# Emitting the engine programs into the main body instead of a Block, in a one-core transformer-block kernel

## The chip, the cores and the metric

One Trainium2 chip, one of its cores. The metric is the device time of one execution in microseconds (us). The "span" of a trace is shorter: from the first to the last instruction of the kernel that the profiler recorded. Both numbers exist for every timed run.

## The reference, cut to what matters

A block with adaptive layer norm: linear attention, then a SwiGLU feed-forward, on 2048 rows of 1024 features in bfloat16.

```python
mod = (silu(c) @ w_mod)                # six rows: sa, ca, ga, sb, cb, gb
h = layernorm(x) * (1 + ca) + sa
x = x + ga * linear_attention(h, A_wqkv, A_wo)
h = layernorm(x) * (1 + cb) + sb
x = x + gb * ((silu(h @ w_gate) * (h @ w_up)) @ w_down)   # 1024 -> 3584 -> 1024
```

The arithmetic is not touched by the change. The last result is stored to memory in small pieces, and the kernel must not be over before the last piece has landed.

## The kernel before

The kernel first records all operations in a list and works out the semaphore waits between them. It then emits one program per engine:

```python
    def emit(self, sems, engines):
        for eng, ops in self.by_eng.items():
            deco = engines[eng]

            def body(e, ops=ops, eng=eng):
                for op in ops:
                    for k, v in op.waits:
                        e.wait_ge(sems[k], v)
                    if op.fn is None:
                        continue
                    r = op.fn(e)
                    ...            # cut: semaphore increments
            deco(body)
```

The `deco` of each engine comes from a Block. A Block gives every engine a body of its own, to which it branches, and joins all five engines behind an all-engine barrier at its end:

```python
    with ExitStack() as es:
        block = es.enter_context(nc.Block())
        ...                        # cut: tiles and the whole list of operations
        P.wait_for("sp", out_ops)  # SyncE waits for all 33 stores

        counters = P.resolve()
        sems = {}
        for key in counters:
            sems[key] = es.enter_context(nc.semaphore(key.replace(":", "_")))
        engines = {"pe": block.tensor, "act": block.scalar, "dve": block.vector, "pool": block.gpsimd,
                   "sp": block.sync}
        P.emit(sems, engines)
```

The last row tile is finished in three pieces so that little is left after the last matmul. The last piece is 128 columns wide: one addition on VectorE, then a store of 128 x 256 bytes.

```python
                        if c0 > 0:
                            P.dve("tensor_tensor", out=xs, in0=PS[:, pb, c0:c1], in1=xs, op=ALU.add)
                        ...        # cut: the wider pieces
                        out_ops.append(P.dma("out", ov[:, st, nh * 512 + c0:nh * 512 + c1], xs))
```

## Time and profile before

| | before |
|---|---|
| time, median of the first three runs | 831.32 us |
| span of the traced run | 829.4 us |
| TensorE busy | 824.0 us, 99% |
| start of the last matmul | 826.60 us |
| issue of the last store | 827.17 us |
| last landing of that store | 828.67 us |
| end of the span | 829.44 us |

The head of the profile page of the kernel before gives the span, the number of instructions and each engine's busy time with its share of the span and its number of instructions:

```profile
span 829.4 us, 10017 instructions
## 1 busy us (share of the span) xinstructions
PE 824.0 (99%) x4083; PEld 378.4 (46%) x4083; DVE 312.0 (38%) x665; ACT 197.6 (24%) x336; POOL 39.8 (5%) x57
...
```

TensorE is the limit and it hardly ever pauses. The chain of waits that ended last (start, duration, what) shows what stands before and after its work:

```profile
...
1.71 4.21 DMA xres<-in_A_x_dram
...
8.76 818.08 PE ps L176 x4069
826.83 0.02 issue
826.86 0.29 DVE xres L176
```

There are 8.76 us of lead-in, one unbroken block of matmuls, and a tail. The waits of SyncE in the last microseconds of the kernel before (who waited for whom: us in total, times, longest) say what the tail is:

```profile
...
engine line waited for: us in total, times, longest us
...
SPq L286 <- DMA out_dram<-xres: 1.2, 1, 1.2
SPq L286 <- PEq L286: 0.5, 1, 0.5
```

SyncE waits 1.2 us for the last store, and then 0.5 us more in the Block's closing barrier. (The releaser's name is a guess of the profile: the barrier is released by GpSimd, as the records below show.) The view of the DMA traffic from 827.1 us to the end of the span (packets, MB and share of the 16 engines per queue; then KB and us from issue to landing of the stores issued in it) has a store that lands in 1.5 us:

```profile
...
## 3 DMA queue, kind: packets, MB, share of 16 engines
q1 hardware_dynamic: 288, 0.13, 19.3%
issues: line engine op xcount, KB each, median us to landing
out_dram<-xres SPq DMA_DIRECT2D x1, 32.0 KB, 1.5
```

The single instruction records at the end of the trace, shortened (start us, duration us, engine, record):

```
827.174  0.333  SyncE    issue of the last store
828.684  0.041  SyncE    branch, after the wait for all stores
828.865  0.013  SyncE    drain, counts up the gather semaphore
828.903  0.017  GpSimd   gather complete
829.334  0.017  GpSimd   release
829.376  0.017  SyncE    released; the others up to 829.439
```

### The profile page before, as it was taken

How to read it: one execution, taken by the hardware profiler on the slowest of the kernel's cores; microseconds unless marked ns; L12 is line 12 of the kernel's file. 1: busy time of each engine (PE TensorE's matmuls, PEld its weight loads, DVE VectorE, ACT ScalarE, POOL GpSimd, SP SyncE). 2: the span in 40 equal slices, each digit the busy share in tenths (PEclk: the TensorE clock that was granted, in tenths of full speed). 3: DMA queues.
4: the chain of work that ended last, by engine and by line, in shares of the span. 5: the costliest groups of instructions: out<-in, count | busy, mean ns of one | idle time of the engine just before them, and what ended most of it. 6: DMA issues, size and time to landing. Idle time of an engine off the chain costs nothing.

```text
span 829.4 us, 10017 instructions
## 1 busy us (share of the span) xinstructions
PE 824.0 (99%) x4083; PEld 378.4 (46%) x4083; DVE 312.0 (38%) x665; ACT 197.6 (24%) x336; POOL 39.8 (5%) x57
## 2 busy tenths in 40 slices
PE   8999999999999999999999999999999999999998
PEld 4544444454444444444444444444444444444444
DVE  5797986756955521121221111122111111221111
ACT  4757641323242111011111101111110111111011
POOL 1010000000130000030000003000000300000000
PEclk9999999999999999999999999999999999999999
DMA  9969655928397996700455570045557004553000
GB/s 320 288 151 229 149 159 172 202 102 304 60 258 225 259 267 174 192 25 14 128 150 155 150 188 28 15 126 153 153 153 187 26 18 125 154 151 86 0 26 26
DMA packets 199245, 119.28 MB, mean 144 GB/s; under 512 B 57880, under 2 KB 182944, under 8 KB 199200
## 3 DMA queue, kind: packets, MB, share of 16 engines
q1 hardware_dynamic: 199184, 118.65, 52.7%
q8 instruction: 32, 0.52, 0.3%
q14 instruction: 13, 0.11, 0.0%
q10 hardware_dynamic: 16, 0.00, 0.0%
HBM read 100.67 MB, written 4.33 MB: 127 GB/s over the span
## 4 chain that ended last, share of the span: by engine, by line
PE 99%; DMA 1%; DVE 0%; ACT 0%; SPq 0%; issue 0%
PE ps L176 99%; DMA xres<-in_A_x_dram 1%; DVE stats L176 0%; ACT xres L176 0%; SPq L176 0%; DVE xres L176 0%; DVE mv L176 0%; DVE nmr L176 0%
## 5 line engine op out<-in xcount | busy, mean ns | idle before, releaser
L176 PE MATMUL ps<-h2t,gug 128*128 128x512 bf16 x896 | 211.7, 379 | 0.0
L176 PE MATMUL ps<-h2t,guu 128*128 128x512 bf16 x896 | 211.7, 379 | 0.0
L176 DVE TENSOR_TENSOR at<-sg,ps 128x512 bf16<-128x512 bf16 x112 | 77.1, 688 | 282.7 <-PE ps L176 281.1
L176 ACT ACTIVATE sg<-ps 128x512 bf16<-128x512 f32 x112 | 66.9, 597 | 309.7 <-PE ps L176 309.7
L176 PEld LDWEIGHTS ps<-h2t,guu 128*128 128x128 bf16 x896 | 87.5, 98 | 105.8
L176 PEld LDWEIGHTS ps<-h2t,gug 128*128 128x128 bf16 x896 | 87.4, 98 | 105.7
L176 PE MATMUL ps<-wd_a,at 128*128 128x512 bf16 (+1 forms) x512 | 112.4, 378 | 0.0
L176 PE MATMUL ps<-ht,wqk 128*128 128x512 bf16 x512 | 111.7, 379 | 0.0
L176 PE MATMUL ps<-wd_b,at 128*128 128x512 bf16 (+1 forms) x384 | 85.0, 378 | 0.0
L176 PEld LDWEIGHTS ps<-wd_a,at 128*128 128x128 bf16 x512 | 50.0, 98 | 59.8
L176 DVE TENSOR_TENSOR ut<-att,gb_b 128x512 bf16<-128x512 bf16 (+1 forms) x32 | 13.8, 430 | 167.5 <-ACT att L176 167.5
L176 PEld LDWEIGHTS ps<-ht,wqk 128*128 128x128 bf16 x512 | 49.4, 98 | 58.8
L176 ACT ACTIVATE att<-ps 128x512 bf16<-128x512 f32 (+1 forms) x32 | 17.4, 591 | 182.1 <-PE ps L176 182.1
L176 PEld LDWEIGHTS ps<-wd_b,at 128*128 128x128 bf16 x384 | 37.5, 98 | 44.7
L176 PE MATMUL ps<-pk,xres 128*128 128x512 bf16 x256 | 56.5, 379 | 0.0
L176 PE MATMUL ps<-mw,pqt 128*128 128x512 bf16 x256 | 56.3, 379 | 0.0
L176 POOL TENSOR_SCALAR h2t<-h2t,modcol 128x512 bf16<-128x512 bf16 x32 | 26.4, 841 | 383.0 <-DMA h2t<-xn 383.0
L176 ACT ACTIVATE e<-ps 128x512 bf16<-128x512 f32 x56 | 33.1, 603 | 31.7 <-PE ps L176 20.5
L176 PEld LDWEIGHTS ps<-mw,pqt 128*128 128x128 bf16 x256 | 24.8, 98 | 30.3 <-DVE xres L176 0.4
L176 PEld LDWEIGHTS ps<-pk,xres 128*128 128x128 bf16 x256 | 24.8, 98 | 30.0 <-issue 0.4
L176 ACT ACTIVATE junk<-xres 128x1024 bf16<-128x1024 bf16 x24 | 25.4, 1058 | 35.1 <-DVE xres L176 34.9
L176 DVE SCALAR_TENSOR_TENSOR xres<-ps,xres 128x512 bf16<-128x512 f32 x32 | 21.4, 689 | 12.3 <-PE ps L176 11.7
(107 smaller groups left out, 346.0 us busy)
## 6 DMA issues: line engine op xcount, KB each, us to landing
gug<-in_B_w_gate_dram SPq DMA_DIRECT2D x56, 512.0 KB, 3.9
guu<-in_B_w_up_dram SPq DMA_DIRECT2D x56, 512.0 KB, 5.2
xres<-in_A_x_dram SPq DMA_DIRECT2D x20, 256.0 KB, 7.8
rb<-recip_den SPq DMA_DIRECT2D x8, 512.0 KB, 11.5
stgx<-in_w_mod_dram SPq DMA_DIRECT2D x2, 2048.0 KB, 7.8
wd_a<-in_B_w_down_dram SPq DMA_DIRECT2D x4, 1024.0 KB, 7.8
out_dram<-xres SPq DMA_DIRECT2D x31, 128.0 KB, 1.7
xres<-in_A_x_dram SPq DMA_DIRECT2D x3, 1024.0 KB, 14.0
```

The source lines that it names most:

```text
L176: return getattr(e, method)(**kw)
```

## The change

The intent: drop the Block, so that there is no branch into a body, no branch out of it, and above all no all-engine barrier at the end. SyncE's wait for all stores, which was already there, becomes the end of the kernel.

```diff
@@ emit
-            deco(body)
+            body(deco)
@@ kernel
-        block = es.enter_context(nc.Block())
@@ end
-        engines = {"pe": block.tensor, "act": block.scalar, "dve": block.vector, "pool": block.gpsimd,
-                   "sp": block.sync}
+        engines = {"pe": nc.tensor, "act": nc.scalar, "dve": nc.vector, "pool": nc.gpsimd, "sp": nc.sync}
```

Compared engine by engine, the programs are the same except for the branches and the barrier.

## The prediction

> **What bounds the kernel now.** TensorE. The profile page gives PE 824.0 us busy of a span of 829.4 us (99%) at a granted clock of 1.0, and the chain that ended last is 818.08 us of matmuls without a break (8.76 to 826.83 us), with 8.76 us of lead-in (a load of x, its statistics and normalisation) and 2.61 us of tail. The time of a run (831.32 us) is 1.9 us more than the span. The change can touch only lead-in, tail and those 1.9 us.
>
> **What the change does.** The order of instructions, compared engine by engine, is the same apart from names: no load, matmul, wait or store moves. What goes is (a) one branch per engine on entry, (b) one on exit, (c) one all-engine barrier at the end: a drain and a semaphore wait on four engines, a drain, a gather and a release on POOL. Next to nothing is added: SyncE already waits for all stores before; that wait is carried by its exit branch, and becomes a plain semaphore wait.
>
> **Cost of each, from the instruction records of the trace.**
> - Entry: no branch is recorded. SyncE's start-up semaphore wait is at 0.703 us and its first DMA issue at 0.785 us, so at most some 0.05 us can hide there; the start-up barrier stays. [...] This trace shows no such stall at entry, so I count 0.
> - Exit: the last store is issued at 827.174 us and SyncE's branch runs at 828.684 us, when the store has landed. Then come the branch (0.041 us), SyncE's drain at 828.865, POOL's gather at 828.903, POOL's release at 829.334, and the other engines' waits, the last ending at 829.439. After landing that is 0.755 us, all on the critical path. A plain wait takes 0.02 to 0.04 us (such records take 0.017 to 0.041). Saved: about 0.72 us.
> - The other engines' drains end by 827.20 us: off the path.
> - [...] SyncE still comes last to it, so I expect it unchanged, a few tenths either way. No view of this trace shows it.
>
> **Prediction.** 831.32 - 0.72 = 830.6 us, 0.09% faster; range 830.1 to 831.1 us. Faster by over 2%: 0.002; within 2%: 0.995; slower by over 2%: 0.003. The three runs before differ by 0.23 us, so the gain is only just visible.
>
> **What the profile would show.** Instruction count 10017 falls by 11 to 10006. The barrier's records at the end are gone; the last record is SyncE's semaphore wait right after the last store lands, so the tail shrinks from 2.6 to about 1.9 us. Span about 828.7 us. The block of matmuls stays 818.1 us within 0.3 us, the lead-in 8.8 us within 0.3 us. Time minus span stays about 1.9 us.
>
> **What would make it wrong.** The runtime's end takes back what the barrier gave (time minus span grows by 0.7 us: no gain), or starts its work early on the idle engines (gain over 0.72 us). The start-up loads land differently by some tenths, which moves the whole block. Instruction fetches shift by a few instructions on every engine; TensorE could gain or lose a fraction of a us.

The 1.9 us between the span and the time (831.32 - 829.4) are the "it" to which SyncE "still comes last". That they follow SyncE was the assumption; the trace shows only that SyncE is the last engine to end its work (its branch at 828.684 us, the other engines' drains over by 827.20 us). "The runtime's end", and "the runtime's end code" in the expectations, are names for whatever comes behind the kernel.

## The result, and the profile after

The changed kernel is correct. Its median is 831.59 us (830.65 to 831.82, 6 runs), against 831.22 us (830.89 to 831.43, 6 runs) for the kernel before. A ratio in this document is the one recorded with each result, made from the fast runs; it is not quite the ratio of the medians. Here it is 1.0002, with a 95% interval from 0.9989 to 1.0015: the same. The predicted 0.7 us are not there.

The head of the page, and the chain, of the changed kernel:

```profile
span 830.2 us, 10006 instructions
## 1 busy us (share of the span) xinstructions
PE 824.5 (99%) x4083; PEld 378.9 (46%) x4083; DVE 312.5 (38%) x665; ACT 197.5 (24%) x336; POOL 40.1 (5%) x57
...
```

```profile
...
8.79 12.47 DMA wsa<-in_w_mod_dram
21.26 0.04 issue
21.31 806.13 PE ps L176 x3932
827.44 0.02 issue
827.46 0.29 DVE xres L176
```

The 11 instructions are gone, as predicted (ten of the barrier and SyncE's exit branch; no other branch is recorded). The span, however, grew from 829.4 to 830.2 us. The block of matmuls ends 0.61 us later (827.44 instead of 826.83 us). Matched one by one, its matmuls are 0.64 us ahead of the kernel before at 8 us and 0.61 us behind from 46 us on: 0.44 us of this is lost at 21 us, where they wait for a load (`wsa`), and the rest in several smaller steps. The tail should have shrunk from 2.61 us to about 1.9 us; it grew to 2.79 us (830.23 - 827.44). SyncE's waits at the end show where:

```profile
...
engine line waited for: us in total, times, longest us
...
SPq L247 <- DMA out_dram<-xres: 2.1, 1, 2.1
```

The barrier's wait is gone, but the wait for the last store went from 1.2 to 2.1 us. The DMA traffic from 827.7 us to the end of the span:

```profile
...
q1 hardware_dynamic: 288, 0.13, 17.8%
q14 instruction: 1, 0.01, 0.9%
issues: line engine op xcount, KB each, median us to landing
out_dram<-xres SPq DMA_DIRECT2D x1, 32.0 KB, 2.4
```

There is a guest: one packet on q14, an instruction fetch, and the same 32 KB store now takes 2.4 us to land. A close-up of the changed kernel from 828.95 to 829.55 us, in 40 slices of 15 ns (bytes are counted where a packet starts):

```profile
...
GB/s 0 0 0 546 0 0 0 0 0 0 0 0 0 0 0 0 0 0 0 0 0 0 0 0 0 0 0 17 17 17 17 17 17 17 17 0 0 0 0 0
DMA packets 10, 0.01 MB, mean 17 GB/s; under 512 B 9, under 2 KB 9, under 8 KB 9
...
```

The fetch starts in the fourth slice. Nothing starts in the next 23. Then come exactly eight packets of the store, one per slice. The ninth packet under 512 B is one of 4 bytes; a store has 16 of these, as it has 16 landings. The packet records give the numbers:

```
                                       before           changed
first packet of the last store         828.001          828.609
instruction fetch, 8192 bytes, q14     830.057-830.550  829.003-829.364
last packets of the last store         no gap           8 of 128 from 829.361
15th and 16th of its 4-byte packets    828.241, .262    828.868, 829.474
15th of the store's 16 landings        828.654          829.254
16th landing                           828.668          830.199
```

Eight of 128 packets are one sixteenth of the store. Fifteen of the sixteen landings are on time, and the last comes 0.95 us after the fifteenth. In the kernel before, a fetch of the same size came too, but at 830.06 us, after the barrier and outside the span. The times fit a fetch that stands in the way of these packets: eight packets wait until 3 ns before the fetch ends (829.361 and 829.364 us), one of the 16 landings is late, and SyncE's wait ends only after it (the wait's record is at 830.215 us, the 16th landing at 830.199 us). The trace does not name the DMA engine of a packet, so that fetch and packets shared one is inferred from these times, and one time does not quite fit (see "What stays open").

A third thing changed: time minus span fell from 1.78 us (831.22 - 829.44) to 1.25 us (831.48 - 830.23), and it is low in every run of the changed kernel (1.22 to 1.32 us in six runs).

So the difference of the two traced runs, +0.26 us (831.48 - 831.22), is the sum of four terms:

| term | before | changed | difference |
|---|---|---|---|
| start to the issue of the last store | 827.17 | 827.78 | +0.61 |
| issue to last landing | 1.49 | 2.42 | +0.92 |
| last landing to end of span | 0.77 | 0.03 | -0.74 |
| end of span to end of time | 1.78 | 1.25 | -0.53 |

### The profile page after: what moved, and what is told of

Same layout as the page of the kernel before. It is cut to its first block, busy times and chain, and to the rows that moved or that the text cites. A ratio compares the mean times of both kernels' runs of the same rounds, so it can differ in the third digit from the quotient of the medians.

```text
span 830.2 us, 10006 instructions
## 1 busy us (share of the span) xinstructions
PE 824.5 (99%) x4083; PEld 378.9 (46%) x4083; DVE 312.5 (38%) x665; ACT 197.5 (24%) x336; POOL 40.1 (5%) x57
## 4 chain that ended last, share of the span: by engine, by line
PE 97%; DMA 2%; SPq 1%; issue 0%; DVE 0%
PE ps L176 97%; DMA wsa<-in_w_mod_dram 2%; SPq L176 1%; DVE xres L176 0%
```

## The experiments

All kernels gave correct results. Each was timed in five rounds beside the kernel before on the same chip, and one run of each was traced. The time from the start to the last store's issue scatters by about 1 us from trace to trace, whatever the end of the kernel looks like. So the most telling number is what follows that issue.

Main theory, "collision": with no barrier to hold the idle engines, one of them runs on into the code behind the kernel, and its instruction fetch takes a DMA engine that still has its share of the last store to move. Rival, "chance": landings of a store scatter, and the fetch is a bystander. A second question is which engine fetches. I first thought ScalarE, because its program seemed to end close before a fetch boundary: in the trace of the changed kernel fetches of 8192 bytes start after the 65th, 193rd, 320th and 448th of ScalarE's 560 records (at 47.90, 121.84, 307.37 and 583.40 us), about 128 apart, so the next would be due some 16 records past its end. (That these four are ScalarE's is inferred from the spacing; the trace does not name a fetch's engine.)

The table collects all traces: us from the issue of the last store to its last landing; from there to the end of the span; from there to the end of the time; and the sum. The last column is where the last small instruction fetch (q14) came, relative to the issue of the last store.

| kernel | landing | span end | time end | sum | fetch |
|---|---|---|---|---|---|
| before | 1.49 | 0.77 | 1.78 | 4.05 | +2.88 |
| changed | 2.42 | 0.03 | 1.25 | 3.70 | +1.22 |
| rep_after | 2.46 | 0.03 | 1.25 | 3.75 | +1.30 |
| end_barrier | 1.50 | 0.62 | 1.80 | 3.93 | +2.71 |
| hold_all | 1.49 | 0.08 | 2.11 | 3.68 | +3.03 |
| hold_act | 1.50 | 0.04 | 1.62 | 3.16 | +2.77 |
| hold_dve | 2.38 | 0.05 | 1.38 | 3.81 | +1.15 |
| hold_pool | 1.48 | 0.04 | 2.14 | 3.66 | +3.04 |
| hold_pe | 1.49 | 0.08 | 1.74 | 3.31 | +2.94 |
| pad_act | 2.41 | 0.03 | 1.25 | 3.69 | +1.08 |
| pad_pool | 1.48 | 0.03 | 1.25 | 2.76 | none near |
| rep_pad_pool | 1.48 | 0.03 | 1.25 | 2.76 | none near |
| pad_pool128 | 2.43 | 0.03 | 1.26 | 3.72 | +1.27 |
| before_pad_pool | 1.48 | 0.42 | 1.72 | 3.62 | none near |

### rep_after: the changed kernel again

No edit.

> The changed kernel again, for a second trace. Collision theory (with nothing to hold the idle engines, one runs on into the code behind the kernel, and its 8192-byte instruction fetch occupies one DMA engine while that engine still has its sixteenth of the last store to move): a fetch on q14 again starts some 1.0 to 1.5 us after the last store's issue, one of the 16 landings of that store comes about 0.9 us after the other 15, and the last wait ends about 2.4 us after the issue of the last store. Chance theory (landings of a store just scatter): the wait ends about 1.5 us after the issue, as in the kernel before. Time minus span 1.25 us in both.

Measured: median 830.89 us against 831.27 us of before, ratio 0.9994 (0.9980 to 1.0007). The fetch came again, 1.30 us after the issue; 15 landings by 829.144 us and the 16th at 830.131 us. So the collision repeats. Only the start differed enough to give another median.

### end_barrier: the barrier back, still no Block

```diff
         P.emit(sems, engines)
+        nc.all_engine_barrier()
```

> The changed kernel with an all-engine barrier added at the end, still without a Block. If entry is free and only the end matters: like the kernel before, that is the last store lands 1.5 us after its issue, about 0.75 us of barrier after it, time minus span about 1.8 us, the q14 fetch after the end of the span, and the time within 0.3 us of the kernel before. If the removed entry branches matter: TensorE's block of matmuls keeps the changed kernel's later start (last matmul at 827.4 us) and the time stays some 0.4 us over that of before.

Measured: median 831.72 us against 831.27 us, ratio 1.0002 (0.9989 to 1.0014). SyncE's waits at the end of this kernel:

```profile
...
SPq L247 <- DMA out_dram<-xres: 1.2, 1, 1.2
SPq L1173 <- PEq L1173: 0.5, 1, 0.5
```

These are the two lines of the kernel before. The landing takes 1.50 us, and time minus span is 1.80 us. SyncE's first DMA issue is at 0.785 us, as in the kernel before, and at 0.786 us in the changed kernel. (That the last matmul starts at 826.59 us, before at 826.60 us, is luck: this time scatters by about 1 us.) So what the change does lies in the closing barrier, but for the exit branch; the entry branches are worth nothing that can be seen. The exit branch is worth about 0.12 us: SyncE's drain comes 0.06 us after its wait here (828.682 to 828.741), and 0.18 us after its branch began in the kernel before (828.684 to 828.865).

### hold_all: no barrier, but nobody may run on

```diff
         P.wait_for("sp", out_ops)
+        for e in ("pe", "act", "dve", "pool"):
+            P.wait_for(e, out_ops)
```

(In the kernel these are four lines.)

> The changed kernel with TensorE, ScalarE, VectorE and GpSimd each also waiting for all stores as their last instruction: no gather and release, but nobody can run ahead. Collision theory: the fetch comes after the landing, the store lands 1.5 us after its issue, the span ends within 0.1 us of the landing (about 0.72 us shorter than with the barrier), time minus span goes back to about 1.8 us, and the time is about 0.7 us under that of before. Chance theory: the landing scatters as in the changed kernel. If idle engines' running ahead saved nothing outside the span: time minus span stays at 1.25 us.

Measured: median 830.84 us against 831.27 us, ratio 0.9994 (0.9981 to 1.0007). The landing is back at 1.49 us, and the fetch comes after it (3.03 us after the issue). The span ends 0.08 us after the landing, as the collision theory wanted. But time minus span rose to 2.1 us (2.04 to 2.16 in five runs), more than the 1.8 us expected. Of the 0.72 us expected, the end gives 0.37 us (4.05 - 3.68). So the time outside the span depends on when the engines end their programs: 1.25 us with SyncE alone held until the landing (the changed kernel's trace), 2.11 us with all five held.

### hold_act, hold_dve, hold_pool, hold_pe: one engine held

```diff
         P.wait_for("sp", out_ops)
+        P.wait_for("act", out_ops)     # or "dve", "pool", "pe"
```

> The changed kernel with ScalarE alone also waiting for all stores. If ScalarE makes the colliding fetch (its fetches are 128 instructions apart, and the next one falls some 15 instructions past its end), or stands before the fetching engine in the runtime's end code: the fetch moves behind the landing, the store lands 1.5 us after its issue, and the time is about 0.9 us under the changed kernel's colliding runs. If another engine makes it and does not depend on ScalarE: the fetch stays about 1.2 us after the issue of the last store and the wait still ends 2.4 us after it.

> The changed kernel with VectorE alone also waiting for all stores. Holding ScalarE alone moved the fetch behind the landing. If ScalarE fetches and stands first in the runtime's end code, holding VectorE changes nothing there: fetch at about 1.2 us after the issue of the last store, 16th landing 0.9 us late, wait ends 2.4 us after the issue. If the fetch (which came 1.2 to 1.3 us after VectorE's last instruction in both traces of the changed kernel) comes only once VectorE too has reached the end code, it moves behind the landing here as well: wait ends 1.5 us after the issue, span ends with it, time minus span about 1.6 us.

> The changed kernel with GpSimd alone also waiting for all stores; GpSimd has been idle since 650 us and is the other engine that may be near a fetch boundary. If GpSimd makes the fetch, it moves behind the landing (wait ends 1.5 us after the issue of the last store). If ScalarE makes it and does not need GpSimd: still 2.4 us and the late 16th landing.

> The changed kernel with TensorE alone also waiting for all stores. Holding ScalarE or GpSimd moved the fetch behind the landing, holding VectorE did not; in the colliding traces the fetch came 1.4 to 1.65 us after TensorE's last matmul. If GpSimd reaches its fetch only after TensorE has reached the end code: the fetch moves behind the landing, wait ends 1.5 us after the issue of the last store. If TensorE does not matter: fetch about 1.2 us after the issue, wait ends 2.4 us after it.

Measured: medians 830.71 (hold_act, before 831.27), 830.95 (hold_dve, before 831.52), 830.63 (hold_pool, before 831.52) and 830.43 us (hold_pe, before 831.35). The ratios are 0.9990, 0.9996, 0.9990 and 0.9991, with intervals that all contain 1. The traces are clearer. The DMA traffic from just before the last store to the end of the span, for hold_act and then for hold_dve:

```profile
...
q1 hardware_dynamic: 288, 0.13, 28.7%
issues: line engine op xcount, KB each, median us to landing
out_dram<-xres SPq DMA_DIRECT2D x1, 32.0 KB, 1.5
```

```profile
...
q1 hardware_dynamic: 288, 0.13, 18.0%
q14 instruction: 1, 0.01, 1.0%
issues: line engine op xcount, KB each, median us to landing
out_dram<-xres SPq DMA_DIRECT2D x1, 32.0 KB, 2.4
```

Holding ScalarE, GpSimd or TensorE moves the fetch behind the landing (2.77, 3.04 and 2.94 us after the issue), and the store lands in 1.5 us. Holding VectorE does not (1.15 us), and eight packets wait again (a gap from 828.093 to 828.556 us, the fetch ending at 828.560 us). So in these runs the fetching engine gets to its fetch only when TensorE, ScalarE and GpSimd have all arrived in the code behind the kernel. It is one of the three, but the holds alone cannot say which. The holds also price being late: time minus span is 1.27 us when only SyncE is late (the changed kernel), and 1.35 with VectorE, 1.63 with ScalarE, 1.76 with TensorE and 2.12 us with GpSimd held as well (means of five runs). In the last three the fetch, too, comes after the landing, and what part of the price is the fetch's was not separated.

### pad_act and pad_pool: move the fetch instead

Nothing is held at the end. The code of one engine is made 24 instructions longer, at a place where that engine is idle, so that the boundary at which it fetches falls elsewhere.

```diff
                 if ch == 0 and ft < 8:
                     macc(STGX[1], ft)
+                if ch == 3 and ft == 0:
+                    for _ in range(24):
+                        P.add("act", lambda e: e.drain(), tag="pad")    # or "pool"
```

> The changed kernel with 24 drains added to ScalarE's program at the start of the last chunk's FFN, where ScalarE is idle four fifths of the time; they shift its code by 24 instructions and nothing is held at the end. Collision theory with ScalarE fetching at every 128th instruction: the fetch falls inside the kernel, before its last activations, none near the last store; the store lands 1.5 us after its issue, the span ends within 0.04 us of it, time minus span is 1.25 us or less, and from the issue of the last store to the end of the time it takes about 2.8 us instead of 4.05 (before) and 3.7 (changed): about 1.2 us under before. If another engine fetches: nothing moves, 3.7 us.

> The same 24 drains in GpSimd's program instead: the placebo if ScalarE makes the fetch (wait ends 2.4 us after the issue of the last store, one landing 0.9 us late, 3.7 us to the end of the time), and the cure if GpSimd makes it (1.5 us and 2.8 us).

Measured: here my belief in ScalarE fell. pad_act did move a fetch of ScalarE into the kernel (to 803.65 us), but the colliding one stayed, at 828.265 us. Its landing took 2.41 us; median 830.87 us against 831.52 us, ratio 0.9993 (0.9980 to 1.0005). The placebo was the cure. pad_pool: median 829.83 us against 831.52 us, ratio 0.9979 (0.9966 to 0.9991). This is the first kernel whose interval excludes 1. The DMA traffic of pad_pool at its end, and then from 649.7 to 652 us, where the drains run:

```profile
...
q1 hardware_dynamic: 288, 0.13, 28.2%
issues: line engine op xcount, KB each, median us to landing
out_dram<-xres SPq DMA_DIRECT2D x1, 32.0 KB, 1.5
```

```profile
...
## 3 DMA queue, kind: packets, MB, share of 16 engines
q14 instruction: 1, 0.01, 1.0%
```

The fetch left the end of the kernel and turned up beside GpSimd's drains, at 650.83 us. At that time GpSimd has nothing more to do, and no store is waited for. It is GpSimd that fetches. From the issue of the last store to the end of the time it now takes 2.76 us, instead of 4.05 us (before) and 3.70 us (changed).

### pad_pool128: as many drains as lie between two fetches

The same edit with `range(128)`.

> The changed kernel with 128 drains in GpSimd's program instead of 24. With 24 the fetch on q14 came at 650.8 us, beside the 13th drain. Collision theory, fetches at every 128th instruction: one fetch again beside the 13th drain at about 650.8 us, the next 128 instructions later, which is again in the runtime's end code: the collision returns, wait ends 2.4 us after the issue of the last store, 3.7 us from that issue to the end of the time. If the drains themselves and not the place of the boundary made the gain: 1.5 us and 2.7 us as with 24.

Measured: one fetch at 651.36 us beside the drains, and another at 828.52 us, again in the store's way. Eight packets wait until 828.824 us, the fetch ending at 828.827 us:

```profile
...
q14 instruction: 1, 0.01, 0.8%
issues: line engine op xcount, KB each, median us to landing
out_dram<-xres SPq DMA_DIRECT2D x1, 32.0 KB, 2.4
```

The median is 830.99 us against 831.35 us, ratio 1.0000 (0.9987 to 1.0014). So it is not the drains that help, but the place of the boundary; and GpSimd's boundaries are 128 instructions apart: 128 more instructions give one more fetch and put the next one back in its old place (1.27 us after the issue, in the changed kernel 1.22 us). TensorE's fetches are larger and further apart: 16384 bytes each, on q8, 253 to 260 TensorE records apart in the last 200 us of the trace of before.

### before_pad_pool: the same padding with the Block kept

The 24 drains in GpSimd's program, in the kernel before.

> The kernel before, with its Block and its barrier, and the same 24 drains in GpSimd's program. Without the Block they gave about 0.9 us by taking the fetch off the last store; in the kernel before the fetch came after the barrier, outside the span. If that fetch (0.3 to 0.5 us) delays the runtime's end code: the time minus span falls from 1.80 to about 1.4 us, the span stays. If it is hidden there: 1.80 us and the time of before within 0.3 us. In no case should it reach the time of the changed kernel with the drains (about 1.4 us under before).

Measured: median 830.72 us against 831.35 us, ratio 0.9994 (0.9981 to 1.0007). Time minus span is 1.73 us (mean of five runs; before 1.78 us in the same rounds), so outside the span the fetch had cost next to nothing (0.05 us). Something else got shorter that I had not expected, SyncE's wait in the barrier:

```profile
...
SPq L286 <- DMA out_dram<-xres: 1.1, 1, 1.1
SPq L286 <- PEq L286: 0.2, 1, 0.2
```

GpSimd's step from gather to release took 0.43 us in the kernel before (828.903 to 829.334) and takes 0.08 us here (828.816 to 828.899), as the start-up barrier's does (0.583 to 0.661 us in the trace of before). No DMA packet stands in that gap of the kernel before. But the records show that the pause belongs to a place in GpSimd's code and not to the barrier. Without drains it stands between the second and the third recorded instruction after the place where the drains go in (there the gather and the release, 0.43 us from start to start, and 0.41 us in end_barrier). In all four kernels with drains in GpSimd's program it stands between the second and the third drain (0.40 to 0.42 us from start to start), while from the fourth on they follow each other in 0.06 us. Each time a q14 fetch is recorded 0.69 to 0.99 us after the pause. So the pause goes with the boundary; that GpSimd waits there for its fetch is likely, but was not tested by itself. With the Block kept, the padding leaves 3.62 us at the end. Without the Block it leaves 2.76 us.

### rep_pad_pool: the version that beats both, again

No edit against pad_pool.

> The changed kernel with 24 drains in GpSimd's program once more, on this job's chip: collision theory: no fetch within 30 us of the end, wait ends 1.5 us after the issue of the last store, time minus span 1.25 us, time about 1.3 us (0.15%) under that of before. If the gain was chance: within 0.5 us of before.

Measured, on another chip: median 829.92 us against 831.35 us, ratio 0.9984 (0.9972 to 0.9997). No fetch near the end, landing 1.48 us, time minus span 1.25 us. The changed kernel with GpSimd's fetch moved away is about 0.2% faster than the kernel before.

## Why the prediction was wrong

The number was wrong: 830.6 us predicted with a range up to 831.1, and 831.59 us measured. Two things came together. The end brought 0.35 us instead of 0.72 us, and in the traced run the last store was issued 0.61 us later. With the first alone that run would have taken about 830.87 us (831.22 - 0.35); rep_after, with the same collision, had a median of 830.89 us. So that the number fell outside the range was in part bad luck with the start; the mechanism failed in both runs. Point by point:

- **What bounds the kernel; what moves; entry.** Right. TensorE is the limit before and after, 11 instructions went, and the first DMA issue (0.785 us before, 0.786 us after) shows that the entry branches cost nothing that can be seen.
- **The barrier's own cost.** Right. Predicted 0.72 us after the landing, measured 0.74 us (0.77 to 0.03 us). Some 0.35 us of it was GpSimd's pause at its boundary (before_pad_pool).
- **"The other engines' drains end by 827.20 us: off the path."** This is the step that failed. It is true of the drains, but the barrier behind them did a second thing: it kept the idle engines from running on. Without it GpSimd's next fetch is recorded 1.2 us after the last store's issue, and the store's last landing comes after 2.42 instead of 1.49 us. That is 0.92 us, more than the barrier had cost. hold_act, hold_pool and hold_pe take it away by holding; pad_pool takes it away without holding; and pad_pool128 brings it back.
- **"SyncE still comes last to it, so I expect it unchanged, a few tenths either way."** The direction was left open and the size was too small. Time minus span fell by 0.53 us in the traced runs, and about as much in the other runs. The holds show that it depends on which engines come late with SyncE. The prediction named as a risk that the end "starts its work early on the idle engines"; the fetch, 1.22 instead of 2.88 us after the last store's issue, fits that. It also named fetches that shift, but thought of TensorE's time alone. What fills this time was not shown; measured is that it took 1.25 to 2.14 us in the traces.
- **"The block of matmuls stays 818.1 us within 0.3 us, the lead-in 8.8 us within 0.3 us."** Too narrow. The first block matmul came at 8.12 us instead of 8.76 us, but several stalls up to 46 us (0.44 us of them for the load of `wsa`) cost 1.25 us, and the last matmul started 0.61 us later. In rep_after nothing is lost after the block's start, which is itself 0.50 us late, so `wsa` is not the rule. Across the 14 traces it starts anywhere from 826.21 to 827.21 us. Neighbours in that scatter have unlike ends: end_barrier at 826.59 and pad_act at 826.61 us; hold_act at 827.07 and rep_after at 827.10 us.
- **"The three runs before differ by 0.23 us, so the gain is only just visible."** Three runs were too few. The 33 timed runs of the kernel before lie between 830.67 and 832.60 us. A gain of 0.35 us at the end (4.05 - 3.70; with rep_after 0.30), which is what the change brought by the traces, is inside that scatter. So the change is not without effect: it gave 0.74 us in the barrier and 0.53 us behind the span, lost 0.92 us to the collision, and the rest could not be told from the start's scatter.

What stays open. The runs show that the place of GpSimd's boundary decides whether the landing is late; how it holds a DMA engine is inferred. The trace does not name the DMA engine. In the nine traces without a collision all packets of the last store have started by 1.09 us after its issue. The fetch's record starts 1.08 us (pad_act) to 1.30 us after it, so the eight packets were already overdue, or just due, when it began: either the fetch held the DMA engine before its packet is recorded, or something else at the same boundary did. And after the waiting packets had gone (829.478 us) the late landing took another 0.72 us (0.72 to 0.74 us in all five colliding traces), while 0.40 us passed between last packet and last landing in the kernel before (828.266 to 828.668); the extra 0.3 us is unexplained.

## What to carry to other kernels

A closing barrier holds the idle engines as well as the last one: with it GpSimd's fetch came 2.88 us after the last store's issue (before) and 2.71 us (end_barrier), without it 1.22 us after (changed). Before removing it, ask what the freed engines do next: here GpSimd fetched code behind the kernel, and with that fetch the very store that the kernel was waiting for landed 0.92 us late. This happened in each of the five traces in which neither a barrier nor a wait held TensorE, ScalarE or GpSimd and GpSimd's code ended shortly before a boundary. When a small change at the end of a kernel is measured, split the time at the last store's issue, since the scatter of the start hides what happens at the end. And a placebo is worth its run: the padding meant as a control turned out to be the cure.
